# The last output block in two PSUM banks, and its rows stored in other pieces

## The chip, the cores and the metric

The kernel runs on one core of a Trainium2 chip. The metric is the device time of one execution in microseconds (us); lower is better. Three executions of the kernel before took 184.32, 182.17 and 182.27 us: median 182.27, lowest 182.17, highest 184.32. One further execution was taken with the hardware profiler; it is the one whose trace is read here.

A core has a matrix engine (TensorE, in the profile PE for matmuls and PEld for weight loads), three engines for elementwise work (VectorE is DVE, ScalarE is ACT, GpSimd is POOL), a queue engine (SyncE, SP) and 16 DMA engines that move data between the chip's memory and the core's SBUF. TensorE writes to PSUM, eight banks of 2 KB on each of 128 partitions; VectorE or ScalarE copies results from there to SBUF, and a DMA stores them. Each engine works through its own queue in order, and they wait for one another through semaphores. SP and ACT each issue DMAs on a queue of their own: SP's is q1 in the profile, ACT's is q10.

## The reference

Sigmoid attention over 8 batches of 12 heads with 448 positions of 64 elements, and behind it a token mixer over the joined heads (448 x 768 for each batch):

```python
scores = scale * np.matmul(q, k.transpose(0, 1, 3, 2)) - np.log(S)
attn = 1.0 / (1.0 + np.exp(-scores))
x = np.matmul(attn, v)                      # then (B, S, H * D) = (8, 448, 768)
wq = x @ w_q                                # 768 -> 64
wk = x @ w_k
W_tok = scale * np.einsum('bsd,btd->bst', wq, wk)
mixed = np.einsum('bst,btd->bsd', W_tok, x)
out = np.maximum(mixed, 0.0) @ w_out        # 768 x 768
```

All inputs and the output are float32. The kernel computes in bfloat16 and accumulates in float32.

## The kernel before

**Stages.** The work is cut into 24 groups `n`, each one batch `u` with four heads. For a group, q, k and v are loaded as float32 (`load1`), cast to bfloat16 (`cast1`, on POOL, DVE or ACT, line 202 for v), and q and k are turned so that the head's 64 elements lie on partitions. `scores(n, i)` makes one seventh of a group's scores (line 298) and their sigmoid on ACT (line 303); `values(n, i)` multiplies with v (line 320), where each weight load reads 64 columns of the cast v tile. Three groups make up a batch. Then follow the projections (`mlp_wqk`, lines 383 and 395), transposes, the mixer's products (`mlp_tmp`, `mlp_mix`) with the relu, and the output product with `w_out`.

**Output.** Two batches make a pair `w` (0 to 3). The pair's 896 rows are cut into seven blocks `m` of 128 rows. An output row of batch b has the number 7 p + i, with p from 0 to 63 and i from 0 to 6; a block holds two values of i, one on partitions 0 to 63 and one on partitions 64 to 127. So a store of one i takes 64 partitions, and its rows in memory lie 7 rows apart. Three functions write output: `out_pair` (pairs 1 and 2), `out_halves` (tokens I and i, blocks 0 to 2 of the last pair) and `out_chunk` (the others). `out_chunk` makes a block's 768 columns in two halves of 384 (`nb` 0 and 1, `NB` = 384), each in one PSUM bank, by six matmuls over the six slices of 128 of the inner dimension (line 590). A half is made in two calls of three matmuls each: the first leaves its state in `opened`, the second (`part` 1) finishes it, copies the bank to the SBUF tile `o` (line 614, on ACT where the token is o or Q, else on DVE), and after the second half the block is stored by `store`: two DMAs of 64 rows (line 599), the first on SP, the second on ACT in the tail of the kernel (`tail`: all scores are done).

**The last block.** For block 6 of pair 3, `split` holds: each half of 384 columns is stored by itself as soon as it is copied. For its second half, the bank is copied in two parts of 192 columns, one on DVE (line 611) and one on ACT (line 612). Both read the same bank, and the framework makes the second wait for the first. Then both 64-row pieces of 384 columns are stored, one on SP and one on ACT.

**Order.** The order of the work is written out by hand: one letter per step in the string `PLAN`. It ends in sixteen tokens O, o and Q, four for each of the last pair's blocks 3 to 6. `BANKS` is a second string that gives, in the order of the requests, the PSUM banks that each step takes (`bank1`, `bank2`); an assertion at the end wants all of it used. The last eight entries, 2 3 4 5 6 7 0 1, are the eight halves of blocks 3 to 6. `read` records who reads a bank, and with `keep=True` two engines that read one bank stay ordered. The `o` tiles come from a pool of three buffers, so block 6 takes the buffer of block 3 after that block's stores have landed.

**Loads and casts.** `ORDER` lists the loads; a dot or a capital letter marks a cast that goes to DVE or ACT at a place fixed in `PLAN`, the others go to POOL as soon as they may (`pump`). Of the 24 casts of v, 20 run on POOL and four on DVE. The tile of a cast v is laid out as partition, seventh `i`, head pair `b`, 64 elements; the float32 tile it comes from as partition, head pair, seventh, 64 elements.

Of the kernel before, what the change touches and what calls it, by code (L numbers as in the profile page):

```python
# [10 lines left out]
BF16 = mybir.dt.bfloat16  # L11
# [6 lines left out]
def kernel(  # L18
# [12 lines left out]
    nc = tc.nc  # L31
    B, H, S, HD = q.shape
    D = H * HD
    DH = moe_w_q.shape[1]
    assert DH == HD == 64 and S == 448 and D == 768
    P = 128
    NI, NP = 7, 64
    NU = B
    NJ = H // 4
    NC = D // P  # L40
    NB = D // 2
    HALF = (slice(0, 64), slice(64, 128))
# [5 lines left out]
    def pool(name, bufs, **kw):  # L48
        return ctx.enter_context(tc.tile_pool(name=name, bufs=bufs, **kw))
# [3 lines left out]
    p_c16 = pool("c16", 2)  # L53
    p_v16 = pool("v16", 4)
# [24 lines left out]
    )  # L79
    BANKS = BANKS.split()[::-1]  # L80

# [2 lines left out]
    def take(*ids):  # L84
        for b in ids:
            readers[b] = (readers[b][0] + readers[b][1], [])

    def bank2():
        lo, hi = (int(b) for b in BANKS.pop())
        take(lo, hi)  # L90
        assert hi == lo + 1
        return (lo, hi), banks[:, lo : hi + 1], banks16[:, lo : hi + 1]

    def bank1():
        b = int(BANKS.pop())
        take(b)
        return (b,), banks[:, b], banks16[:, b]

    def read(fb, inst, keep=False):

        for b in fb:
            for old in readers[b][0]:
                if not keep and old.ins.engine != inst.ins.engine:
                    tc.declare_no_dep(inst.ins, old.ins, reason="both only read the bank")
            readers[b][1].append(inst)
# [15 lines left out]
    quads = [(u, j) for u in range(NU) for j in range(NJ)]  # L121
    N = len(quads)
    COPY = dict(v=nc.vector.tensor_copy, s=nc.scalar.copy, g=nc.gpsimd.tensor_copy)

    def xt(u, j):
        return xts[u % 2 * NJ + j]
# [20 lines left out]
    ld = {}  # L147
# [39 lines left out]
    def cast1(n, nm, e):  # L187
        if KIND[n] in "cer" and nm != "v":
            if n not in pq:
                pq[n] = p_c16.tile([P, 2, 2, NI, 32, 2], BF16, tag="qk16", name="qk16")  # L190
            f = pq[n]
            COPY[e](  # L192
                out=f[:, :, "qk".index(nm)].rearrange("p e i d y -> p e y i d"),
                in_=ld.pop((nm, n)).rearrange("p (y i e d) -> p e y i d", y=2, i=NI, e=2),
            )
            ld[nm + "16", n] = f
            if ("q16", n) in ld and ("k16", n) in ld:
                arrange(n, nc.gpsimd)
            return
        p = p_v16 if nm == "v" else p_c16  # L200
        t16 = p.tile([P, NI, 2, HD], BF16, tag=nm + "16", name=nm + "16")
        COPY[e](  # L202
            out=t16.rearrange("p i b d -> p b i d"),
            in_=ld.pop((nm, n)).rearrange("p b (i d) -> p b i d", i=NI),
        )
        ld[nm + "16", n] = t16
# [106 lines left out]
    def values(n, i, tail, eng):  # L313
        u, j = quads[n]
        if i == 0:
            pv[n] = bank2()
        fb, ps, _ = pv[n]
        for h in range(2):
            for g in range(2):
                nc.tensor.matmul(  # L320
                    ps[HALF[g], h, 0:S], ld["v16", n][HALF[h], i, g, :],
                    ats[n, i][HALF[h], g, :], start=(i == 0), stop=(i == NI - 1),
                )
        if i == NI - 1:
            if tail:
                for h in range(2):
                    read(fb, COPY["vs"[h]](out=xt(u, j)[:, h, 0:S], in_=ps[:, h, 0:S]))
            else:
                read(fb, COPY[eng](out=xt(u, j)[:, :, 0:S], in_=ps[:, :, 0:S]))  # L329
# [158 lines left out]
    chunks = []  # L488
    ot = {}

    opened = []
# [80 lines left out]
    def out_chunk(act, tail):  # L572

        if opened:
            w, m, nb, fb, ps = opened.pop()
            part = 1
        else:
            w, m, nb = chunks.pop(0)
            if nb < 0:
                nb = 0  # L580
                chunks.insert(0, (w, m, 1))
            fb, ps, _ = bank1()
            part = 0
        if nb == 0 and not part:
            ot[0] = p_o.tile([P, D], F32, tag="o", name="o")
        o = ot[0]

        def block(ps, w0, w1, c0, c1):
            for c in range(c0, c1):
                nc.tensor.matmul(  # L590
                    ps, mxs[w][:, 2 * S * c + m * P : 2 * S * c + (m + 1) * P],
                    wout16[:, c, w0:w1], start=(c == 0), stop=(c == NC - 1),
                )

        def store(cols):
            for y in range(2):
                b, i = divmod(2 * m + y, NI)
                eng = nc.scalar if tail and y else nc.sync
                eng.dma_start(
                    out=out[2 * w + b].rearrange("(p i) d -> p i d", i=NI)[:, i, cols],  # L600
                    in_=o[HALF[y], cols],
                )

        ps = ps[:, 0:NB] if not part else ps
        block(ps, nb * NB, (nb + 1) * NB, part * NC // 2, (part + 1) * NC // 2)
        if not part:
            opened.append((w, m, nb, fb, ps))
            return
        if w == NU // 2 - 1 and not chunks:
            h = NB // 2  # L610
            read(fb, nc.vector.tensor_copy(out=o[:, NB : NB + h], in_=ps[:, 0:h]), keep=True)
            read(fb, nc.scalar.copy(out=o[:, NB + h :], in_=ps[:, h:]), keep=True)
        else:
            read(fb, COPY["s" if act else "v"](out=o[:, nb * NB : (nb + 1) * NB], in_=ps), keep=True)  # L614
        split = tail and w == NU // 2 - 1 and m == NI - 1
        if nb or split:
            store(slice(nb * NB, (nb + 1) * NB) if split else slice(0, D))

    w32 = {}

# [21 lines left out]
    def cols(r):  # L642
        return slice(r.start * HD, r.stop * HD)
# [8 lines left out]
        out=ident, in_=ident, compare_op=ALU.not_equal, fill=1.0, base=0,  # L652
# [8 lines left out]
    for t in wqks:  # L661
        nc.vector.memset(t[:, S:], 0.0)


    ORDER = (
# [4 lines left out]
    )  # L670
    BY = {"s": [], "v": []}
    for x in ORDER.split():
        if x[0] == ".":
# [1 line left out]
        elif x[0].isupper():  # L675
            BY["s"].append((x[0].lower(), int(x[1:])))
    OTHERS = set(BY["s"] + BY["v"])
    ORDER = [(x[0], int(x[1:])) for x in ORDER.replace(".", "").lower().split()]
    done = dict.fromkeys("SPqkKxWNUMOCgz", 0)
    used, loaded, cast = set(), set(), set()  # L680

# [2 lines left out]
    def pump_loads():  # L684
        while len(loaded) < len(ORDER):
            nm, n = ORDER[len(loaded)]
            if nm == "w" and n:
                loaded.add((nm, n))
                continue
            if len(ring) >= 8 and ring[-8] not in cast:  # L690
                break
            ring.append((nm, n))
            if nm == "w":
                load_weights()
            else:
                load1(n, nm, nc.sync)
            loaded.add((nm, n))
# [13 lines left out]
    def cast_now(nm, n, e):  # L711
        if nm != "w":
            cast1(n, nm, e)
        elif n:
            if n % 3 == 1:
                load_wout(n - 1)
        else:
            for h in range(2):
                for g in range(2):
                    COPY[e](  # L720
                        out=wqk16[HALF[g], h::2],
                        in_=w32["qk"].rearrange("p (c n) -> p c n", c=NC)[HALF[h], g::2],
                    )
        cast.add((nm, n))
        pump_loads()
# [3 lines left out]
    def pump():  # L729
        while pumped[0] < len(ORDER):  # L730
            nm, n = ORDER[pumped[0]]
            if (nm, n) not in OTHERS:
                if not ready(nm, n):
                    break
                cast_now(nm, n, "g")
            pumped[0] += 1

    def cast_next(e):
# [7 lines left out]
    for t16, t32, r, e in ((q016, q0, IA, "v"), (q016, q0, IB, "s"), (k016, k0, KA, "g"), (k016, k0, KB, "g")):  # L746
        COPY[e](
            out=t16[:, r].rearrange("p i b d -> p b i d"),
            in_=t32[:, :, cols(r)].rearrange("p b (i d) -> p b i d", d=HD),
# [23 lines left out]
    for t in PLAN:  # L773
# [9 lines left out]
        tail = done["S"] == N * NI  # L783
        if t == "S":
            scores(*divmod(c, NI))
        elif kind == "P":
            n, i = divmod(c, NI)
            values(n, i, tail or t == "R", "s" if t == "p" else "v")
            if i == NI - 1:
                used.add(("v", n))  # L790
                pump()
# [13 lines left out]
        elif t == "z":  # L805
            n = quads_r.pop(0)
# [16 lines left out]
        elif kind == "M":  # L823
            u, x = divmod(c, NC // 2)
# [44 lines left out]
```

## Time and profile before

| | |
|---|---|
| median of 3 runs | 182.27 us |
| the profiled execution's own time | 182.05 us |
| its span, first to last instruction | 180.3 us |
| granted TensorE clock, mean | 0.996 |
| TensorE, ScalarE, VectorE, GpSimd busy | 169.6, 160.0, 142.1, 123.4 us |
| last matmul of the run, end (modelled) | 176.13 us |
| read from memory, written to memory | 35.78 MB, 11.01 MB |

The span is some 1.8 us shorter than the time of the same execution; the rest lies ahead of the first and behind the last instruction. Busy shares are means over the whole run. The chain of waits goes back from the last instruction, at each step to what released it. For a DMA the profile has the time at which its queue issued it, the time until its data had landed, and for each queue the packets: one for each row moved and some small ones that report completion.

### The profile page before, as it was taken

Reading aid. Unit: us, or ns where it says so; the run is one execution under the profiler, and the core shown is the slowest. Engines: PE = TensorE matmul, PEld = TensorE weight load, DVE = VectorE, ACT = ScalarE, POOL = GpSimd, SP = SyncE. Lnnn points to the kernel's source line nnn. Section 1 sums busy time; section 2 is a strip of 40 time slices with the busy share of each in tenths; the row PEclk is TensorE's granted clock in tenths of the full one; section 3 lists DMA queues with packets and bytes.
Section 4 is the critical chain, followed back from the end, with each engine's and each line's share of the span. In section 5 each row is a group of like instructions: output and inputs, shape, how many; then the busy total and the mean of one; then the engine's idle time right before and its main releaser. Section 6 shows DMA issues by size and latency. Waiting matters only on the chain.

```text
span 180.3 us, 7970 instructions
## 1 busy us (share of the span) xinstructions
PE 169.6 (94%) x3471; PEld 112.5 (62%) x3472; DVE 142.1 (79%) x229; ACT 160.0 (89%) x212; POOL 123.4 (68%) x168
## 2 busy tenths in 40 slices
PE   7787899889999999999999999999999999999990
PEld 7333555554455445655686768778987789778560
DVE  3239599998989899889899879887999866588810
ACT  4699999999999999999999989999999899985240
POOL 1397799998998999999999999989306990000000
PEclk9999999999999999999999999999999999999998
DMA  5999999999999799989998999983946744442686
GB/s 174 356 394 387 331 382 376 288 302 364 411 340 346 181 306 292 372 285 288 313 282 285 281 374 346 316 266 96 264 118 155 226 95 107 91 91 46 157 241 175
DMA packets 24915, 47.31 MB, mean 262 GB/s; under 512 B 3888, under 2 KB 18480, under 8 KB 24880
## 3 DMA queue, kind: packets, MB, share of 16 engines
q1 hardware_dynamic: 23680, 44.84, 77.0%
q0 software_dynamic: 800, 1.18, 3.6%
q10 hardware_dynamic: 400, 0.79, 1.4%
q8 instruction: 27, 0.44, 1.0%
q14 instruction: 8, 0.07, 0.1%
HBM read 35.78 MB, written 11.01 MB: 260 GB/s over the span
## 4 chain that ended last, share of the span: by engine, by line
PE 67%; DVE 14%; DMA 9%; POOL 4%; SPq 2%; ACT 2%; issue 2%
PE banks L298 13%; PE banks L320 13%; PE banks L590 13%; PE banks L509 11%; DVE qk L232 4%; DMA k<-in_k_dram 4%; DMA v<-in_v_dram 3%; PE banks L549 3%; PE banks L395 3%; DVE xt L329 3%; POOL qk L192 3%; PE banks L358 2%; DVE qk L256 2%; DVE xn L347 1%; DMA out_dram<-o 1%
## 5 line engine op out<-in xcount | busy, mean ns | idle before, releaser
L303 ACT ACTIVATE at<-banks 128x896 bf16<-128x896 f32 x168 | 140.9, 946 | 3.6 <-PE banks L298 2.7
L298 PE MATMUL banks<-qk 64*64 64x448 bf16 x672 | 62.5, 357 | 2.5 <-DVE xt L329 1.4
L320 PE MATMUL banks<-at,v 64*64 64x448 bf16 x672 | 46.5, 350 | 0.1
L298 PEld LDWEIGHTS <-qk 64*64 64x64 bf16 x672 | 25.8, 105 | 21.1 <-issue 12.5
L509 PE MATMUL banks<-wout,mx 64*64 64x384 bf16 x672 | 36.3, 323 | 0.0
L320 PEld LDWEIGHTS <-v 64*64 64x64 bf16 x672 | 23.7, 106 | 6.9 <-issue 0.8
L509 PEld LDWEIGHTS <-mx 64*64 64x64 bf16 x672 | 23.3, 107 | 4.3
L590 PE MATMUL banks<-wout,mx 128*128 128x384 bf16 x132 | 24.8, 327 | 0.0
L192 POOL CAST qk<-q 128x896 bf16<-128x896 f32 x19 | 22.6, 1191 | 0.7 <-DMA q<-in_q_dram 0.2
L450 DVE TENSOR_SCALAR mx<-banks 128x512 bf16<-128x512 f32 (+3 forms) x24 | 21.0, 882 | 2.4 <-PE banks L477 1.6
L161 POOL COPY swap<-qk 32x448 uint32<-32x448 uint32 x28 | 15.8, 564 | 10.2 <-DVE qk L192 8.5
L192 POOL CAST qk<-k 128x896 bf16<-128x896 f32 x18 | 21.5, 1194 | 1.8 <-POOL qk L167 0.9
L329 DVE CAST xt<-banks 128x896 bf16<-128x896 f32 x19 | 20.5, 1081 | 1.4 <-PE banks L320 1.0
L202 POOL CAST v<-v 128x896 bf16<-128x896 f32 x20 | 18.4, 931 | 0.6
L590 PEld LDWEIGHTS <-mx 128*128 128x128 bf16 x132 | 11.9, 98 | 10.7 <-issue 3.9
L164 POOL COPY qk<-qk 32x448 uint32<-32x448 uint32 x28 | 16.6, 592 | 1.6
L263 DVE STREAM_TRANSPOSE qk<-qk 128x448 f32<-128x448 f32 x28 | 17.3, 630 | 0.1
L167 POOL COPY qk<-swap 32x448 uint32<-32x448 uint32 x28 | 15.8, 564 | 1.6
L232 DVE STREAM_TRANSPOSE qk<-qk 32x448 f32<-32x448 f32 x24 | 15.3, 636 | 0.6
L371 DVE COPY xn<-banks 128x1024 bf16<-128x1024 bf16 (+1 forms) x17 | 11.1, 654 | 4.6 <-PE banks L358 4.6
L614 DVE COPY o<-banks 128x384 f32<-128x384 f32 x15 | 8.2, 550 | 1.6 <-PE banks L590 0.8
L358 PEld LDWEIGHTS <-xt 64*64 64x64 bf16 x544 | 7.6, 109 | 1.9 <-issue 1.0
(87 smaller groups left out, 196.2 us busy)
## 6 DMA issues: line engine op xcount, KB each, us to landing
q<-in_q_dram SPq DMA_DIRECT2D x24, 448.0 KB, 7.0
v<-in_v_dram SPq DMA_DIRECT2D x24, 448.0 KB, 6.3
k<-in_k_dram SPq DMA_DIRECT2D x23, 448.0 KB, 7.3
out_dram<-o SPq DMA_DIRECT2D x51, 192.0 KB, 3.5
wout<-in_moe_w_out_dram POOLq DMA_DIRECT2D x2, 576.0 KB, 12.1
wout<-wout SPq DMA_DIRECT2D x12, 96.0 KB, 5.2
out_dram<-o ACTq DMA_DIRECT2D x3, 192.0 KB, 3.4
k<-in_k_dram SPq DMA_DIRECT2D x1, 256.0 KB, 5.2
```

The lines of the kernel that those rows point to most:

```text
L164: eng.tensor_copy(out=w[hi, 0], in_=w[lo, 1])
L192: COPY[e](out=f[:, :, "qk".index(nm)].rearrange("p e i d y -> p e y i d"), in_=ld.pop((nm, n)).rearrange("p (y i e d) -> p e y i d", y=2, ...
L202: COPY[e](out=t16.rearrange("p i b d -> p b i d"), in_=ld.pop((nm, n)).rearrange("p b (i d) -> p b i d", i=NI),)
L232: nc.vector.transpose(out=qk[n][other : other + 32, h].rearrange("p t i n -> p (t i n)").bitcast(F32), in_=w[own : own + 32, 1 - h],)
L263: nc.vector.transpose(out=qk[n][:, t].rearrange("p t i n -> p (t i n)").bitcast(F32), in_=w)
L298: nc.tensor.matmul(sc[HALF[h], g, 0:S], qk[n][HALF[g], h, 1, i, :], qk[n][HALF[g], h, 0].rearrange("p i n -> p (i n)"), start=True, stop=True,
L303: inst = nc.scalar.activation(at, sc[:, :, 0:S], ACTF.Sigmoid, bias=attn_bias, scale=attn_scale)
L320: nc.tensor.matmul(ps[HALF[g], h, 0:S], ld["v16", n][HALF[h], i, g, :], ats[n, i][HALF[h], g, :], start=(i == 0), stop=(i == NI - 1),)
L329: read(fb, COPY[eng](out=xt(u, j)[:, :, 0:S], in_=ps[:, :, 0:S]))
L450: inst = nc.vector.tensor_scalar(dst, ps, moe_scale, 0.0, ALU.mult, ALU.max)
L509: nc.tensor.matmul(ps[HALF[x], y, 0:NB], mx[HALF[y], u, b, 64 * (i - 3 * y) : 64 * (i - 3 * y) + 64], wout16[HALF[y], slot(y, b), x * NB : ...
L590: nc.tensor.matmul(ps, mxs[w][:, 2 * S * c + m * P : 2 * S * c + (m + 1) * P], wout16[:, c, w0:w1], start=(c == 0), stop=(c == NC - 1),)
```

## The change

The tile of a cast v is now laid out as partition, head pair, seventh, 64 elements, as its source is. `cast1` writes it in one run, and line 320 reads it with the two indices exchanged. `cast1` also gets a way to load v with a DMA that casts, for entries of `ORDER` marked with a star. No entry has a star, so it isn't used.

The last block's second half takes two banks: the string `BANKS` gets one more entry, 2. Its first call makes columns 384 to 575 with all six slices, and its second call columns 576 to 767 with all six. DVE copies the first bank, ACT the second, without waiting for each other.

The stores of the last block's rows: columns 0 to 383 and columns 384 to 575 are each stored by one DMA on SP for all 128 partitions (`store_both`), whose destination counts the two values of i, then 64 rows, then the columns. Columns 576 to 767 are stored by two DMAs of 64 rows, on SP and on ACT. In all, ACT issues one store fewer and SP one more; the order of all other instructions on all engines is as before.

```diff
-        "45 01 67 45 01 2 3 4 5 6 7 0 1 "
+        "45 01 67 45 01 2 3 4 5 6 7 0 1 2 "
...
-        p = p_v16 if nm == "v" else p_c16
-        t16 = p.tile([P, NI, 2, HD], BF16, tag=nm + "16", name=nm + "16")
+        if nm == "v":
+            t16 = p_v16.tile([P, 2, NI, HD], BF16, tag="v16", name="v16")
...
+                COPY[e](
+                    out=t16.rearrange("p b i d -> p (b i d)"), in_=ld.pop((nm, n)).rearrange("p b x -> p (b x)"),
+                )
+            ld["v16", n] = t16
+            return
...
-                    ps[HALF[g], h, 0:S], ld["v16", n][HALF[h], i, g, :],
+                    ps[HALF[g], h, 0:S], ld["v16", n][HALF[h], g, i, :],
...
+        last = w == NU // 2 - 1 and m == NI - 1
+
+        def store_both(cols):
+
+            b, i = divmod(2 * m, NI)
+            nc.sync.dma_start(
+                out=out[2 * w + b].rearrange("(p i) d -> i p d", i=NI)[i : i + 2, :, cols], in_=o[:, cols],
+            )
...
+        if nb and last:
+
+            if part:
+                fb, ps, _ = bank1()
+            h = NB // 2
+            c0 = NB + part * h
+            block(ps[:, 0:h], c0, c0 + h, 0, NC)
+            read(fb, COPY["vs"[part]](out=o[:, c0 : c0 + h], in_=ps[:, 0:h]), keep=True)
+            if part:
+                store(slice(c0, D))
+            else:
+                store_both(slice(c0, c0 + h))
+                opened.append((w, m, nb, fb, ps))
+            return
...
-        if w == NU // 2 - 1 and not chunks:
-            h = NB // 2
-            read(fb, nc.vector.tensor_copy(out=o[:, NB : NB + h], in_=ps[:, 0:h]), keep=True)
-            read(fb, nc.scalar.copy(out=o[:, NB + h :], in_=ps[:, h:]), keep=True)
-        else:
-            read(fb, COPY["s" if act else "v"](out=o[:, nb * NB : (nb + 1) * NB], in_=ps), keep=True)
-        split = tail and w == NU // 2 - 1 and m == NI - 1
-        if nb or split:
-            store(slice(nb * NB, (nb + 1) * NB) if split else slice(0, D))
+        read(fb, COPY["s" if act else "v"](out=o[:, nb * NB : (nb + 1) * NB], in_=ps), keep=True)
+        if last:
+            store_both(slice(0, NB))
+        elif nb:
+            store(slice(0, D))
```

More of the change, by code (lines that the diff above doesn't have):

```diff
@@ L199, in cast1 @@
             return
-        p = p_v16 if nm == "v" else p_c16
-        t16 = p.tile([P, NI, 2, HD], BF16, tag=nm + "16", name=nm + "16")
+        if nm == "v":
+            t16 = p_v16.tile([P, 2, NI, HD], BF16, tag="v16", name="v16")
+            if e == "d":
+                u, j = quads[n]
+                nc.gpsimd.dma_start(
+                    out=t16.rearrange("p b i d -> p b (i d)"),
+                    in_=v[u, 4 * j : 4 * j + 4].rearrange("(g h) (p i) d -> (h p) g (i d)", g=2, i=NI),
+                )
[5 more added lines that the diff above has]
+            return
+        t16 = p_c16.tile([P, NI, 2, HD], BF16, tag=nm + "16", name=nm + "16")
         COPY[e](
@@ L593, in block @@
                 )
+        last = w == NU // 2 - 1 and m == NI - 1
[3 more added lines that the diff above has]
+                out=out[2 * w + b].rearrange("(p i) d -> i p d", i=NI)[i : i + 2, :, cols], in_=o[:, cols],
+            )
         def store(cols):
@@ L602, in store @@
                 )
+        if nb and last:
[7 more added lines that the diff above has]
+                store(slice(c0, D))
+            else:
+                store_both(slice(c0, c0 + h))
+                opened.append((w, m, nb, fb, ps))
+            return
         ps = ps[:, 0:NB] if not part else ps
@@ L677 @@
     OTHERS = set(BY["s"] + BY["v"])
-    ORDER = [(x[0], int(x[1:])) for x in ORDER.replace(".", "").lower().split()]
+    CASTING = {("v", int(x[2:])) for x in ORDER.split() if x[0] == "*"}
+    ORDER = [(x[0], int(x[1:])) for x in ORDER.replace(".", "").replace("*", "").lower().split()]
     done = dict.fromkeys("SPqkKxWNUMOCgz", 0)
@@ L686, in pump_loads @@
             nm, n = ORDER[len(loaded)]
-            if nm == "w" and n:
+            if nm == "w" and n or (nm, n) in CASTING:
                 loaded.add((nm, n))
@@ L734, in pump @@
                     break
-                cast_now(nm, n, "g")
+                cast_now(nm, n, "d" if (nm, n) in CASTING else "g")
             pumped[0] += 1
```

## The prediction

> **What bounds the kernel now.** I read the page first, for the engine that fills the span.
>
> ```profile
> span 180.3 us, 7970 instructions
> ...
> PE 169.6 (94%) x3471; PEld 112.5 (62%) x3472; DVE 142.1 (79%) x229; ACT 160.0 (89%) x212; POOL 123.4 (68%) x168
> ...
> q10 hardware_dynamic: 400, 0.79, 1.4%
> ```
>
> TensorE is busy for 94% of the span, so in the middle of the run only something that delays or feeds TensorE counts. The change touches the end, so next comes the chain of waits, its last five pieces (start, duration, what):
>
> ```profile
> 168.21 7.92 PE banks L590 x48
> 176.13 0.02 issue
> 176.15 0.37 DVE o L611
> 176.52 0.02 issue
> 176.54 0.32 ACT o L612
> ```
>
> The last 48 matmuls run back to back, 7.92 / 48 = 0.165 us each. Then VectorE and ScalarE copy the two halves of one PSUM bank one after the other. After that only stores are left. When they are issued is in ScalarE's timeline and in line 599's own answer (durations in ns, first and last start):
>
> ```profile
> 175.38 0.48 ACT L614 COPY o<-banks 128x384 f32<-128x384 f32 x1 [0.70 <-DMA out_dram<-o]
> 175.89 0.50 ACTq L599 DMA_DIRECT2D out_dram<-o  x1
> ```
>
> ```profile
> L599 SPq DMA_DIRECT2D out_dram<-o x1: 467/467/467, 176.9 to 176.9; - x1
> L599 ACTq DMA_DIRECT2D out_dram<-o x1: 497/497/497, 176.9 to 176.9; - x1
> ```
>
> Both queues issue a 64-row piece of the left half at 175.89 and of the right half at 176.89. The DMA answers for 177.0 to 177.5 and 177.5 to 178.0 show how long those take to land, and what the queues moved:
>
> ```profile
> DMA packets 75, 0.17 MB, mean 335 GB/s; under 512 B 14, under 2 KB 27, under 8 KB 75
> ...
> q10 hardware_dynamic: 58, 0.15, 82.5%
> q1 hardware_dynamic: 17, 0.02, 11.0%
> issues: line engine op xcount, KB each, median us to landing
> out_dram<-o SPq DMA_DIRECT2D x1, 96.0 KB, 2.2
> out_dram<-o ACTq DMA_DIRECT2D x1, 96.0 KB, 2.5
> ```
>
> ```profile
> DMA packets 126, 0.16 MB, mean 320 GB/s; under 512 B 22, under 2 KB 126, under 8 KB 126
> ...
> q10 hardware_dynamic: 61, 0.08, 46.3%
> q1 hardware_dynamic: 65, 0.08, 44.2%
> ```
>
> The last piece lands at 176.89 + 2.5 = 179.39, and the span ends 0.9 us later. So the set end is: copies, an issue, 2.5 us of DMA, 0.9 us of closing. The stages by time agree; their last two columns are the share of 16 DMA engines and GB/s:
>
> ```profile
> 178.00:179.00 1.00, 0.00 (x0) 0.00 (x0) 0.00 (x0) 0.00 (x0) 0.00 (x0) 0.94 0.70 214
> 179.00:180.30 1.30, 0.00 (x0) 0.00 (x0) 0.00 (x0) 0.00 (x0) 0.00 (x0) 0.50 0.00 0
> ```
>
> Data moves until about 179.0, and 0.4 us later the last piece has landed.
>
> **The change, part by part.** The sum is made against the profiled execution, 182.05 us around its span of 180.3; the median of the runs, 182.27, is 0.22 above it.
>
> *The v tile.* The 24 casts of v now write one run of 896 elements where they wrote fourteen of 64. The groups, shapes kept apart (busy us, mean ns of one | idle):
>
> ```profile
> L202 POOL CAST v<-v 128x896 bf16<-128x896 f32 x20 | 18.4, 931 | 0.6
> ...
> L202 DVE CAST v<-v 128x896 bf16<-128x896 f32 x4 | 2.8, 696 | 0.0
> ...
> L404 POOL COPY wq<-wqk 64x448 bf16<-64x448 bf16 x4 | 2.2, 555 | 0.2
> ...
> L747 POOL CAST k<-k 128x512 bf16<-128x512 f32 x1 | 0.6, 613 | 1.7 <-DMA k<-in_k_dram 1.7
> ```
>
> On POOL a copy in one run (555 ns for 448) and a cast in runs of 64 (613 for 512) lie on a line with the 931 for 896: 613 + 384 x (613 - 555) / 64 = 961. The shape of the run does not show in the price, so I take nothing; the 30 ns between line and row, twenty times, is 0.6 us either way, on an engine with 57 us to spare. VectorE's four casts could gain at most a part of 4 x 0.70 = 2.8 us, beside TensorE's work; nothing taken. TensorE's weight loads still read 64 elements in a row.
>
> *The last 384 columns.* Six matmuls of 384 columns become twelve of 192, with six more weight loads. Nothing of 192 columns was run; the nearest below is the transposes of 128 columns with the same 128 x 128 load:
>
> ```profile
> 38.35 0.57 PE banks L342 x8
> ```
>
> That is 0.071 us each. By columns twelve cost 12 x 0.165 / 2 = 0.99 us, exactly the old six; by the line through 0.071 and 0.165 they cost 12 x 0.0945 = 1.13. So 0 to +0.15; I take +0.07. Bank 2, the second bank, was emptied by the row block three before, so its wait costs nothing.
>
> *The copies.* VectorE's 0.37 us now lies under the second six matmuls, and ScalarE's 0.32 follows TensorE directly: 176.13 + 0.07 + 0.02 + 0.32 = 176.54 instead of 176.86. That is 0.32 us earlier, and the ScalarE queue issues its last piece, now 64 x 192, at 176.57.
>
> *The stores.* ScalarE's issue at 175.89 goes (0.50 us of its queue, which waited for nothing). On SP three follow one another: 2 x 64 rows of 384 columns after the copy that ends at 175.86, 2 x 64 rows of 192 columns after VectorE's copy (about 176.1), and 64 rows of 192. SP's price for an issue with two dimensions beside the columns:
>
> ```profile
> L563 SPq DMA_DIRECT2D out_dram<-o x6: 595/598/1222, 164.5 to 170.2; - x6
> ```
>
> So the issues start at 175.89, 176.54 and 177.19: the last is 0.30 us later than SP's last was (176.89), and whoever waits for SP is the end of the program alone.
>
> What decides is how the two new stores are carried. Their destination counts 2 rows outermost, then 64, then the columns; every store of before counts 64 outermost. ScalarE's queue shows how such a one is divided: 400 packets for five stores are 80 each, 64 rows and 16 completions, one for each of 16 engines that took four rows. An issue costs SP 0.47 us for 64 rows and 0.60 for 64 x 2, far too little to deal out rows singly, so I take it that the outermost dimension is cut into equal shares. Of two there are two shares: **two engines carry 64 rows each, and 14 stand idle.** No row of this trace has an outermost count below 64, so this is inferred, and its bounds are 16 engines (below) and two.
>
> The Trainium skill states this as a rule (DMA: Bandwidth & Descriptors, section "Why a DMA increments its semaphore by 16 and not by 1"): the number of engines is the largest up to 16 that divides the slowest dimension of both access patterns. For 2 and 128 that is two engines; no run shown so far has tried it.
>
> The price of a row: from 177.5 to 178.0 the two queues took (46.3 + 44.2)% of 16 x 0.5 us = 7.24 us for 126 - 22 = 104 rows of 1,536 bytes, 70 ns each. In the half before, 93.5% of 8 us is 7.48; less 13 such rows, 48 rows of 3,072 bytes took 6.57 us, 137 ns each. The price goes by bytes, 22 GB/s per engine, and the line through both gives 36 ns for 768 bytes. On each of the two engines:
> - the first rows of 1,536 bytes ran between 177.0 and 177.5, after an issue at 175.89 and behind the row block before: start about 177.2
> - 64 x 0.070 = 4.5 us, to 181.7
> - the second store behind it, 64 x 0.036 = 2.3 us, to 184.0
> - its share of SP's last piece, 4 x 0.036 = 0.15, to 184.2
> - 0.4 to landing, 0.9 of closing: the span ends at 185.5.
>
> That is 5.2 us later; the 0.32 us from the copies is lost under it, since the first store's issue at 175.89 has not moved. 182.05 + 5.2 = 187.25, and with the median's 0.22 about **187.5 us**.
>
> Bounds of the row's price: the fastest slice of the page and the store queue alone.
>
> ```profile
> GB/s 174 356 394 387 331 382 376 288 302 364 411 340 346 181 306 292 372 285 288 313 282 285 281 374 346 316 266 96 264 118 155 226 95 107 91 91 46 157 241 175
> ```
>
> ```profile
> q1 hardware_dynamic: 1408, 1.94, 45.4%
> ```
>
> 411 / 16 = 25.7 GB/s puts 147,456 bytes through in 5.7 us instead of 6.8: 186.4. The second line is from 141 to 160 us, where SP alone stores: 45.4% of 16 x 19 us = 138 us for 1.94 MB, 14 GB/s. Then it is 10.5 us, 3.7 more: 191.2. I stay with 22: each of those stores reads 64 partitions with all 16 engines, while two queues over 128 partitions reached 335 GB/s.
>
> **The rivals.**
>
> *Sixteen engines carry the two-row stores as all others.* For it: every store measured used 16. Against it: none had this form. Then the ScalarE queue lands at 176.57 + 2.5 = 179.07 and SP at 177.19 + 2.2 = 179.39, which is the old landing; half the bytes per piece may take 0.2 off. 0 to -0.3: 182.2 us, not slower. It decides if the first store lands within about 3 us.
>
> *Sixteen engines, but the SP queue becomes the bound.* SP carries 344 KB of the last 393. At the 14 GB/s per engine of SP alone, 225 GB/s, these need 1.53 us from 177.2, to 178.7, beneath the 179.39; issues of 0.75 instead of 0.60 would add 0.3. So 182.5 us. In the Trainium skill (DMA: Bandwidth & Descriptors, "Rules for kernel authors") two transfers of disjoint partition halves are said to gain nothing over one of 128 partitions, which by itself would make this merge free; the 335 against 225 GB/s differ from that.
>
> *Two engines at SP's lone rate*: 191.2 us, as worked out. For it: only one queue feeds them. Against: at 3,072 bytes as at 1,536 time went by bytes, so no fixed wait per row shows.
>
> **How the numbers follow.** Two engines at 22 to 26 GB/s, the forecast: 0.68. Two engines near 14 GB/s: 0.13. Sixteen engines: 0.13. SP bound: 0.06. The likeliest gives 187.5. The range takes in the forecast with its bounds (186.4, and 0.5 less if the start and the landing are each somewhat shorter) and most of the slow case: 185.9 to 191.3. Within 2% of 182.27 (up to 185.9, about what a measurement of this kernel can tell from no change) are the two cases of sixteen engines, 0.19, less a hundredth; faster by that much is out of reach of a tail whose copies are worth 0.3 us: 0.01. Slower: 0.80.
>
> **What would show it.** Right: the two two-row stores land after some 6 and 8 us instead of 2.7, the DMA share falls to about 2/16 after 178.5, SP's closing wait for the stores grows from about 1 us to 6 or more, and ScalarE's last copy starts right after TensorE at about 176.2. Wrong: all landings near 2.5 us, or a slowdown that stands ahead of 175.9, where v's new layout would have cost what I put at nothing.

## The result, and the profile after

The changed kernel takes 188.62 us (median of 6 runs, 187.92 to 190.58), the kernel before 182.22 in the same series: a ratio of 1.0349, 95% interval 1.0279 to 1.042. It is slower by 6.4 us. Ratios here and below come from the runs outside a kernel's slower state, so they need not be the quotient of the two medians beside them. The execution that was profiled took 187.92 us, the fastest of the six, 5.87 more than the profiled one of before.

The head of the page of the changed kernel, and its rate of DMA in 40 slices of 4.65 us:

```profile
span 186.1 us, 7984 instructions
...
PE 169.9 (91%) x3478; PEld 113.5 (61%) x3478; DVE 142.7 (77%) x229; ACT 159.8 (86%) x212; POOL 123.9 (67%) x168
...
GB/s 177 397 384 371 350 384 341 302 298 404 386 311 279 271 289 345 312 314 306 302 262 301 327 331 321 284 75 288 105 179 214 95 85 92 88 85 174 238 69 30
```

No engine's busy time has grown by more than 1.0 us (169.6 to 169.9 us on TensorE), and the last two slices move 69 and 30 GB/s where the kernel before ended with 241 and 175. To see that the time is lost in the tail alone, take the start of the last four row blocks' matmuls, first before, then after (start, duration):

```profile
168.14 7.97 PE L590 MATMUL banks<-wout,mx 128*128 128x384 bf16 x48
```

```profile
167.83 7.99 PE L603 MATMUL banks<-wout,mx 128*128 128x384 bf16 x54
```

The changed kernel gets there 0.3 us earlier. From there to the end of the span it is 180.3 - 168.14 = 12.16 us before and 186.1 - 167.83 = 18.27 after: the tail is 6.1 us longer. This length, called the tail below, is what the experiments are read by, since the start of the tail itself moves from run to run: in the traces here it lies between 167.83 and 170.09 us.

The end of the timeline after (start, duration, engine; SPq and ACTq are issues):

```profile
175.08 0.48 ACT L645 COPY o<-banks 128x384 f32<-128x384 f32 x1 [0.70 <-DMA out_dram<-o]
175.37 0.36 DVE L633 COPY o<-banks 128x192 f32<-128x192 f32 x1 [3.65 <-PE banks L603]
175.58 1.24 SPq L613 DMA_DIRECT2D out_dram<-o  x2
175.86 0.32 ACT L633 COPY o<-banks 128x192 f32<-128x192 f32 x1 [0.30 <-PE banks L603]
176.21 0.47 ACTq L621 DMA_DIRECT2D out_dram<-o  x1
176.92 0.70 SPq L621 DMA_DIRECT2D out_dram<-o  x1
```

The copies do what the change says: ScalarE's last one waits for TensorE and starts 0.78 us after its copy of the left half; before it was 1.16 us (176.54 - 175.38). All is issued by 177.6. From there to the end of the span only DMAs run. The stages by time (last two columns: share of 16 engines, GB/s), then the landings of the last small pieces (KB, us from issue to landing) and SP's closing wait:

```profile
177.00:178.00 1.00, 0.00 (x0) 0.00 (x0) 0.00 (x0) 0.00 (x0) 0.00 (x0) 1.00 0.51 48
178.00:179.00 1.00, 0.00 (x0) 0.00 (x0) 0.00 (x0) 0.00 (x0) 0.00 (x0) 0.82 0.60 59
179.00:180.00 1.00, 0.00 (x0) 0.00 (x0) 0.00 (x0) 0.00 (x0) 0.00 (x0) 0.50 0.61 76
180.00:181.00 1.00, 0.00 (x0) 0.00 (x0) 0.00 (x0) 0.00 (x0) 0.00 (x0) 0.50 0.31 56
181.00:182.00 1.00, 0.00 (x0) 0.00 (x0) 0.00 (x0) 0.00 (x0) 0.00 (x0) 0.50 0.13 48
182.00:183.00 1.00, 0.00 (x0) 0.00 (x0) 0.00 (x0) 0.00 (x0) 0.00 (x0) 0.50 0.14 47
183.00:184.00 1.00, 0.00 (x0) 0.00 (x0) 0.00 (x0) 0.00 (x0) 0.00 (x0) 0.50 0.14 48
184.00:185.00 1.00, 0.00 (x0) 0.00 (x0) 0.00 (x0) 0.00 (x0) 0.00 (x0) 0.50 0.06 21
```

```profile
out_dram<-o ACTq DMA_DIRECT2D x1, 48.0 KB, 3.9
out_dram<-o SPq DMA_DIRECT2D x1, 48.0 KB, 8.1
```

```profile
SPq L897 <- DMA out_dram<-o: 7.3, 1, 7.3
```

From 181 to 184 the share is 0.13 to 0.14, and 2/16 is 0.125: two engines at work, with 47 to 48 GB/s together. Between 178 and 180 it is still 0.6, and yet only 59 to 76 GB/s move: the small last pieces, which all engines carry, run slowly there too. SP's last piece, 48 KB, lands at 176.92 + 8.1 = 185.0. It stands behind the two-row stores on two of the engines. SP waits 7.3 us for it at the end, where it was 1.7 in two waits.

### The profile page after: what moved, and what is told of

It reads as the page before. It is cut to its first block, busy times and chain, and to the rows that moved or that the text cites. A ratio compares the mean times of both kernels' runs of the same rounds, so it can differ in the third digit from the quotient of the medians.

```text
span 186.1 us, 7984 instructions
## 1 busy us (share of the span) xinstructions
PE 169.9 (91%) x3478; PEld 113.5 (61%) x3478; DVE 142.7 (77%) x229; ACT 159.8 (86%) x212; POOL 123.9 (67%) x168
## 4 chain that ended last, share of the span: by engine, by line
PE 57%; POOL 15%; DVE 11%; ACT 8%; issue 2%; DMA 2%; SPq 0%; POOLq 0%; DVEq 0%
PE banks L311 11%; PE banks L333 11%; PE banks L522 10%; PE banks L603 10%; ACT at L316 7%; POOL qk L192 5%; DVE qk L245 3%; PE banks L562 3%; POOL swap L161 3%; POOL qk L167 3%; POOL qk L164 2%; DVE xt L342 2%; PE banks L408 2%; PE banks L371 2%; DMA k<-in_k_dram 2%
## 5 line engine op out<-in xcount | busy, mean ns | idle before, releaser
L311 PEld LDWEIGHTS <-qk 64*64 64x64 bf16 x672 | 26.4, 105 | 21.3 <-issue 13.1
L603 PE MATMUL banks<-wout,mx 128*128 128x384 bf16 (+1 forms) x138 | 24.8, 320 | 0.0
```

What stands on the lines that cost most here:

```text
L311: nc.tensor.matmul(sc[HALF[h], g, 0:S], qk[n][HALF[g], h, 1, i, :], qk[n][HALF[g], h, 0].rearrange("p i n -> p (i n)"), start=True, stop=True,
L603: nc.tensor.matmul(ps, mxs[w][:, 2 * S * c + m * P : 2 * S * c + (m + 1) * P], wout16[:, c, w0:w1], start=(c == 0), stop=(c == NC - 1),)
```

## The experiments

The theory: each two-row store is carried by two of 16 engines, since its destination counts 2 outermost. The rivals: the SP queue is the bound, because it issues and carries almost all; the new layout of v costs; the order in which rows reach memory costs.

### The two-row stores taken apart

```diff
...
         def store_both(cols):
-            b, i = divmod(2 * m, NI)
-            nc.sync.dma_start(
-                out=out[2 * w + b].rearrange("(p i) d -> i p d", i=NI)[i : i + 2, :, cols], in_=o[:, cols],
-            )
+            for y in range(2):
+                b, i = divmod(2 * m + y, NI)
+                nc.sync.dma_start(
+                    out=out[2 * w + b].rearrange("(p i) d -> p i d", i=NI)[:, i, cols], in_=o[HALF[y], cols],
+                )
```

> The changed kernel, with each two-row store taken apart into two stores of 64 rows, both on SP; v's layout, the two banks and ScalarE's part stay. If two engines carried the two-row stores: the loss of 6 us goes, and SP's five issues in a row (some 0.5 us each from 175.6) put its last one at about 177.8, some 0.9 us later than in the kernel before; with 2.2 us to land and 0.9 of closing the time is 182.3 to 183.2. If the SP queue with most of the bytes is what costs: still 186 or more, since the same bytes go through the same queue. If v's layout costs: unchanged, 188.

Measured: 183.91 us against 183.3 of before on that chip, ratio 1.0059 (1.002 to 1.0099). The tail is 181.9 - 168.27 = 13.63 us. Of the 6.1 us, 4.6 are gone, with the same bytes still on the SP queue. By the times some 1.1 us over before are left (0.4 to 1.8 by the interval; 0.1 to 1.0 was expected). SP's row of issues fits that:

```profile
176.02 2.66 SPq L614 DMA_DIRECT2D out_dram<-o  x4
178.77 0.55 SPq L622 DMA_DIRECT2D out_dram<-o  x1
```

Its fifth issue starts 2.75 us after its first; before, the second was the last, 1.0 us after the first (176.89 - 175.89). So the rival of the SP queue is worth 1.5 us of tail at most, in this one trace, and it isn't the cause of the 6.

### v's layout alone, and two banks alone

```diff
...
-        t16 = p.tile([P, NI, 2, HD], BF16, tag=nm + "16", name=nm + "16")
+        if nm == "v":
+            t16 = p_v16.tile([P, 2, NI, HD], BF16, tag="v16", name="v16")
...
-                    ps[HALF[g], h, 0:S], ld["v16", n][HALF[h], i, g, :],
+                    ps[HALF[g], h, 0:S], ld["v16", n][HALF[h], g, i, :],
```

> The kernel before with v's tile in the new layout and nothing else. By the prediction: no difference, 182.2 within 0.3, POOL's cast of 896 elements stays at 931 ns within 10. Rival: VectorE's four casts of v, which had a mean of 696 ns before and 858 in the changed kernel, are slower by the layout; then they show 850 again here, and the time may be up to 0.6 us longer.

Measured: ratio 1.0002 (0.9966 to 1.0039), tail 180.5 - 168.37 = 12.13 us against 12.16. No difference shows, within 0.7 us either way.

```profile
L202 POOL CAST v<-v 128x896 bf16<-128x896 f32 x20 | 18.3, 931 | 0.7 <-DMA v<-in_v_dram 0.2
...
L202 DVE CAST v<-v 128x896 bf16<-128x896 f32 x4 | 2.8, 700 | 0.0
```

VectorE's four casts have 700 ns here with the new layout, 858 in the changed kernel, and 849 in the run with one two-row store below, which has the old layout: the spread isn't the layout's.

```diff
-        "45 01 67 45 01 2 3 4 5 6 7 0 1 "
+        "45 01 67 45 01 2 3 4 5 6 7 0 1 2 "
...
+        if nb and last:
+            if part:
+                fb, ps, _ = bank1()
+            h = NB // 2
+            c0 = NB + part * h
+            block(ps[:, 0:h], c0, c0 + h, 0, NC)
+            read(fb, COPY["vs"[part]](out=o[:, c0 : c0 + h], in_=ps[:, 0:h]), keep=True)
+            if part:
+                store(slice(NB, D))
...
```

> The kernel before with the last half of the last block in two PSUM banks and nothing else: the copies run side by side, and the stores are as before (64 rows, 384 columns, one each on SP and ACT). By the working of the prediction the last issue comes 0.3 us earlier, so 181.9 against 182.2, at most 0.4 less, and the wait of ScalarE's last copy is for TensorE and no longer for VectorE. If twelve matmuls of 192 columns cost more than by columns, up to 0.15 of it goes. If the end is set by the DMA engines and not by the last issue: no difference.

> The kernel with two banks and the stores of before once more, since its gain of 0.3 us lay within the uncertainty: a ratio of 0.998 is expected again, with an interval that together with the first tells it from 1 or does not.

Measured: ratios 0.9977 (0.9937 to 1.0016) and 0.9995 (0.9962 to 1.0028); the tails are 182.1 - 170.09 = 12.01 and 181.1 - 168.88 = 12.22 us against 12.16. The tails show no gain of 0.3 us; the times can't tell 0.3 us, or 0.16%, from nothing. ScalarE's timeline in the first of the two shows what became of it:

```profile
177.33 0.48 ACT L627 COPY o<-banks 128x384 f32<-128x384 f32 x1 [0.70 <-DMA out_dram<-o]
177.84 0.50 ACTq L599 DMA_DIRECT2D out_dram<-o  x1
178.38 0.32 ACT L611 COPY o<-banks 128x192 f32<-128x192 f32 x1 [0.57 <-PE banks L590]
```

With the stores of before, ScalarE's own queue issues a piece of the left half between its two copies, until 178.34, and the last copy starts at 178.38, 1.05 us after the first (in the second run it is 1.05 too). Without that issue, in the changed kernel, it was 0.78, before it was 1.16. The profile puts the wait down to TensorE, but the issue ended last. So the wait between the copies hid an issue, and taking the wait away moves the last copy by only 0.1 us unless the issue goes elsewhere too.

A version in which ScalarE copies the first bank and each queue stores 192 columns behind each copy runs into the same issues (its edit, set against the run with two banks):

```diff
...
-            read(fb, COPY["vs"[part]](out=o[:, c0 : c0 + h], in_=ps[:, 0:h]), keep=True)
-            if part:
-                store(slice(NB, D))
+            read(fb, COPY["sv"[part]](out=o[:, c0 : c0 + h], in_=ps[:, 0:h]), keep=True)
+            store(slice(c0, c0 + h))
...
```

> The kernel before with two banks, ScalarE copying the first and VectorE the second, and 64 rows of 192 columns stored from each queue behind each copy. The last stores are issued at about 176.6, 0.3 us earlier than before, and are half as large. If the end follows the last issue: 181.6 to 181.9. If small rows cost the DMA engines more than their bytes (36 ns for 768 bytes was taken), the gain shrinks to none.

Measured: ratio 0.9993 (0.995 to 1.0036), tail 181.6 - 168.92 = 12.68 us, half a microsecond longer, with one issue more on each queue. The 0.3 to 0.6 us that it was expected to win aren't there. No version here beats the kernel before by more than the uncertainty.

### One two-row store, and one on each queue

```diff
...
+            if split and not nb:
+                b, i = divmod(2 * m, NI)
+                nc.sync.dma_start(
+                    out=out[2 * w + b].rearrange("(p i) d -> i p d", i=NI)[i : i + 2, :, 0:NB], in_=o[:, 0:NB],
+                )
+                return
```

> The kernel before with only the left half of the last block in a two-row store on SP; the right half as before. With two engines: 98 KB on each at the 24 GB/s that the changed kernel shows are 4.1 us from about 177.2, then four rows of the last piece, 0.3: data until 181.6, landing and closing 1.3 to 1.5, span 183 and time 184.6 to 185.2. With sixteen engines: 182.2.

Measured: 186.31 against 183.01, ratio 1.0184 (1.013 to 1.0238): 3.3 us for one such store, somewhat above the 2.4 to 3.0 over 182.2 that was expected. Tail 184.4 - 168.41 = 15.99. A two-row store does it with v, the banks and the copies of before.

```diff
-        def store_both(cols):
+        def store_both(cols, eng=nc.sync):
...
-            nc.sync.dma_start(
+            eng.dma_start(
...
-            store_both(slice(0, NB))
+            store_both(slice(0, NB), nc.scalar)
```

> The changed kernel with its first two-row store (384 columns) issued from ACT and the second from SP. If two of the engines carry every two-row store, whichever queue it comes from, the same two have the same 147 KB each: 187.5 to 189, no gain. If one queue's rate is the bound, or each queue has engines of its own, the two stores run side by side: the 2.1 us of the second go, about 186.3. If SP's issue is what costs: about 183.

Measured: 189.04 against 183.01, ratio 1.0311 (1.0237 to 1.0386), as slow as the changed kernel. Tail 187.8 - 169.25 = 18.55. With one two-row store on each queue, two of the late microseconds, and the packets of each queue from 183.0 to 183.5, are:

```profile
183.00:184.00 1.00, 0.00 (x0) 0.00 (x0) 0.00 (x0) 0.00 (x0) 0.00 (x0) 0.50 0.14 50
184.00:185.00 1.00, 0.00 (x0) 0.00 (x0) 0.00 (x0) 0.00 (x0) 0.00 (x0) 0.50 0.13 47
```

```profile
q10 hardware_dynamic: 11, 0.02, 8.9%
q1 hardware_dynamic: 11, 0.01, 5.0%
```

Both queues move rows then, and together they fill 13.9% of 16 engines, about two of them (12.5%): both queues' stores share the same two engines. A queue's own rate isn't the bound.

### The outermost count as the only change

```diff
-                eng.dma_start(
-                    out=out[2 * w + b].rearrange("(p i) d -> p i d", i=NI)[:, i, cols],
-                    in_=o[HALF[y], cols],
-                )
+                dst = out[2 * w + b].rearrange("(p i) d -> p i d", i=NI)[:, i, cols]
+                if tail and w == NU // 2 - 1 and m == NI - 1:
+                    dst = dst.rearrange("(x a) d -> a x d", a=4)
+                eng.dma_start(out=dst, in_=o[HALF[y], cols])
```

Three more runs have 8, 16 and 2 in the place of the 4.

> The kernel before; in the last block's four stores the 64 rows go to memory in another order (so the rows of that block stand at other places), such that the destination counts 4 outermost and then 16. Bytes, queues, issue times and row lengths are those of before. If the outermost count is the number of engines: four engines carry 393 KB, 98 KB each, 4.1 us from about 177.2 at 24 GB/s: span 182.5 to 183, time 184.3 to 185. If the order of rows in memory is what costs, or nothing does: 182.2 to 182.6.

> As the run with 4 outermost, with 8 outermost and then 8. If the outermost count is the number of engines: 49 KB on each of eight, 2.05 us from 177.2, data until about 179.3 instead of 179.0: time 182.3 to 182.9, and in the last microseconds the DMA share does not go above a half. If the count does not matter: as before, with a share of 0.9 or more.

> As the runs with 4 and 8 outermost, with 16 outermost and then 4, so the rows of the last block stand in another order in memory. If the outermost count sets the number of engines: sixteen, and time and DMA share are those of the kernel before (span 180 to 181 from equal ends of TensorE, share 0.9 in the microsecond after the last block's first rows). If the order of the rows in memory costs by itself: longer by 0.5 or more, as with 8.

> The same with 2 outermost and then 32: four stores of 64 rows, two from each queue. All 393 KB of the last block then go through two engines, 197 KB each, 8.2 us at 24 GB/s, and some 1 us for the slow start: data until 186.5, span 187.8 to 188.5, time 189.5 to 190.3. In the last microseconds the DMA share is 0.13 and the rate 48 GB/s.

Each was timed once, so the tail and the late rates tell more than the times. The rates with 2 outermost, with 4, with 8 and with 16, a line or two from each run's stages:

```profile
183.00:184.00 1.00, 0.00 (x0) 0.00 (x0) 0.00 (x0) 0.00 (x0) 0.00 (x0) 0.50 0.13 49
```

```profile
182.00:183.00 1.00, 0.00 (x0) 0.00 (x0) 0.00 (x0) 0.00 (x0) 0.00 (x0) 0.50 0.23 66
183.00:184.00 1.00, 0.00 (x0) 0.00 (x0) 0.00 (x0) 0.00 (x0) 0.00 (x0) 0.50 0.24 88
```

```profile
178.00:179.00 1.00, 0.00 (x0) 0.00 (x0) 0.00 (x0) 0.00 (x0) 0.00 (x0) 0.99 0.40 135
179.00:180.00 1.00, 0.00 (x0) 0.00 (x0) 0.00 (x0) 0.00 (x0) 0.00 (x0) 0.50 0.48 146
```

```profile
178.00:179.00 1.00, 0.00 (x0) 0.00 (x0) 0.00 (x0) 0.00 (x0) 0.00 (x0) 1.00 0.76 258
```

| outermost | time, us | tail, us | late share | count / 16 | GB/s per engine at work |
|---|---|---|---|---|---|
| 2 | 192.18 | 190.4 - 169.68 = 20.72 | 0.13 | 0.125 | 49 / 2 = 24 |
| 4 | 187.53 | 185.8 - 169.38 = 16.42 | 0.24 | 0.25 | 88 / 4 = 22 |
| 8 | 183.61 | 181.8 - 168.11 = 13.69 | 0.48 | 0.5 | 146 / 8 = 18 |
| 16 | 183.0 | 181.2 - 168.97 = 12.23 | 0.76 | 1 | 258 / (0.76 x 16) = 21 |

The same bytes and rows on the same queues: the edits differ in the outermost count alone, and the share of engines at work follows it up to 8; with 16 the last rows no longer keep all engines busy. The packets of ScalarE's queue (q10) over the whole run count the engines directly. With 2, 4, 8 and 16 outermost the pages have:

```profile
q10 hardware_dynamic: 372, 0.79, 1.1%
```

```profile
q10 hardware_dynamic: 376, 0.79, 1.1%
```

```profile
q10 hardware_dynamic: 384, 0.79, 1.2%
```

```profile
q10 hardware_dynamic: 400, 0.79, 1.2%
```

Three of this queue's five stores are unchanged and have 80 packets each, 64 rows and 16 completions. The other two have the rest: 372 - 240 = 132, which is 2 x (64 + 2), then 2 x (64 + 4), 2 x (64 + 8) and 2 x (64 + 16). A store leaves as many completions as its outermost count, and 16 where that is 64; read as the prediction read them, one for each engine that took part.

With 16 the tail is that of before (12.23 against 12.16), though its rows too reach memory in another order, so another order by itself cost nothing there. The Trainium skill's rule (DMA: Bandwidth & Descriptors, section "Why a DMA increments its semaphore by 16 and not by 1"), the largest number up to 16 that divides the slowest dimension of both sides, agrees with all four rows.

With 2, 4 and 8 the times came out 1.9, 2.5 and 0.7 us above the top of what was expected; the kernel before took 183.0 to 183.15 in these series, some 0.8 to 0.9 more than the 182.2 us of the first series, which is one part of it. Another part is ScalarE's issue, which takes 1.35 us with 4 outermost and 0.50 before, ahead of its last copy; that copy starts 1.91 us after the one before it (178.53 - 176.62), where it was 1.16. The rest is not worked out.

```profile
177.13 1.35 ACTq L602 DMA_DIRECT2D out_dram<-o  x1
178.53 0.32 ACT L612 COPY o<-banks 128x192 f32<-128x192 f32 x1 [1.42 <-DVE o L611]
```

### A two-row store with nothing beside it

```diff
-        if nb or split:
-            store(slice(nb * NB, (nb + 1) * NB) if split else slice(0, D))
+        if split:
+            if nb:
+                b, i = divmod(2 * m, NI)
+                nc.sync.dma_start(
+                    out=out[2 * w + b].rearrange("(p i) d -> i p d", i=NI)[i : i + 2, :, :], in_=o,
+                )
+            return
+        if nb:
+            store(slice(0, D))
```

> The kernel before with all 768 columns of the last block in one two-row store on SP, issued when both halves are copied, and nothing behind it on either queue. 64 rows of 3,072 bytes on each of two engines, 128 ns each at 24 GB/s, are 8.2 us from 1.3 after the issue at about 176.9: data until 186.4, span about 187.8, time 189.6. In the runs so far a two-row store moved only half that rate in its first 2 us, while rows of other stores ran on the other engines. If those others hold it up, the rate is 48 GB/s here from the first microsecond on; if such a store always starts slowly, it is again near 25 at first and the time 190.5.

Measured, once: 189.88 us against 183.15 of before, tail 188.1 - 168.07 = 20.03. Its first microseconds, and the packets of SP's queue over the whole run, before and here:

```profile
178.00:179.00 1.00, 0.00 (x0) 0.00 (x0) 0.00 (x0) 0.00 (x0) 0.00 (x0) 0.71 0.15 25
179.00:180.00 1.00, 0.00 (x0) 0.00 (x0) 0.00 (x0) 0.00 (x0) 0.00 (x0) 0.50 0.10 31
180.00:181.00 1.00, 0.00 (x0) 0.00 (x0) 0.00 (x0) 0.00 (x0) 0.00 (x0) 0.50 0.14 43
181.00:182.00 1.00, 0.00 (x0) 0.00 (x0) 0.00 (x0) 0.00 (x0) 0.00 (x0) 0.50 0.12 49
```

```profile
q1 hardware_dynamic: 23680, 44.84, 77.0%
```

```profile
q1 hardware_dynamic: 23650, 45.03, 73.7%
```

On SP two stores of 80 packets went, and one came; 160 - 30 = 130 packets are its 128 rows and 2 completions. No other store is in flight from 178 on, and it still starts at half its later rate. Against 50 GB/s from the first, the three slow microseconds lack 25 + 19 + 7 = 51 KB, 1.0 us. That other stores hold it up is ruled out for this run; why such a store starts slowly stays open.

## Why the prediction was right

187.5 us was forecast and 188.62 measured; on the profiled executions, 5.2 us more against 5.87.

- **Two engines for the two-row stores.** Right, and shown from four sides: taken apart, 4.6 us of tail are gone; one of them alone costs 3.3 us; on two queues they are no faster; and the share and the number of completions follow the outermost count.
- **The price of a row.** 70 ns for 1,536 bytes and 36 for 768 were taken. The late rate of 48 GB/s makes it 1,536 / 24 = 64 ns and 32 ns. The slow case of 14 GB/s, which the queue's rate would have set, fell. The reason given against it was misread, though: in the half microsecond of 335 GB/s ScalarE's queue alone, with stores of 64 partitions, moved 0.15 of the 0.17 MB at 82.5% of the engines, which is 23 GB/s per engine. So reading 64 partitions does not by itself explain SP's 14, and what does stays open.
- **The term that was too small.** The stream was taken to run at full rate from its start. In the lone store it runs at 25, 31 and 43 GB/s in its first three microseconds, where 50 are reached later, and that costs 1.0 us. By the prediction's own clock the tail would have been 185.5 - 168.14 = 17.36, and it was 18.27, 0.9 more. The cheaper rows took 64 x (6 + 4) ns = 0.6 us off, so the sum lacked 1.5: about 1.0 for the slow start, if it is here what it is in the lone store, 0.2 for the closing (186.1 - 185.0 = 1.1 where 0.9 was taken), and 0.3 that is not accounted for. That the forecast came as near as it did is in part luck: two errors of opposite sign met.
- **The copies.** Forecast 0.32 us earlier by ScalarE, measured 1.16 - 0.78 = 0.38, hidden under the stores as forecast. The prediction credits it to the second bank; the run with two banks alone has 1.16 - 1.05 = 0.11, so most of it came from ScalarE's issue of 0.50 us, which was taken to hold up nothing and went to SP. Twelve matmuls of 192 columns cost nothing over six of 384: 54 matmuls in 7.99 us, 48 in 7.97. The allowance of 0.07 wasn't needed.
- **v's layout.** Taken at nothing, and nothing was measured (1.0002, within 0.7 us either way).
- **The SP queue.** Its rival was priced at 0.3 us over the old end; it is up to 1.5 us of tail once SP issues five 64-row stores in a row, and the prediction had three issues there. In the changed kernel it is covered.
- **The signs.** SP's closing wait of 7.3 us and ScalarE's copy right behind TensorE (175.86; the matmuls end at 167.83 + 7.99 = 175.82) came as said. The share of 2/16 came at 181 and not after 178.5: the prediction did not see how slowly ScalarE's last 48 KB would move beside the two-row stores; they took 3.9 us to land, where its last 96 KB took 2.5 before.

## What to carry to other kernels

Before merging two stores into one, look at the outermost count of its destination: here a store that counted 2, 4 or 8 first, with 64 to 8 rows beneath, left 14, 12 or 8 engines idle. (No run here varies the count of the source.) At the end of this kernel nothing hid that. And when a wait is removed, look at what the waiting engine issues in that time: here the wait of 0.3 us hid a DMA issue of 0.5 us, and nothing measurable was won while that issue stayed in its place. No run shows a faster kernel with the issue moved.

## What the runs showed of the hardware that was not expected

The lone two-row store starts slowly: 25, 31 and 43 GB/s in its first full microseconds, 49 to 55 after, with no other store in flight. Whether that comes of the few engines isn't shown. An issue can take longer as well: with 2, 4 or 8 outermost the first of ScalarE's two stores of the last block took 1.32 to 1.41 us to issue, 0.59 with 16, 0.50 before. The second one, of the same shape, took 0.55 to 0.65, so the count alone isn't the reason. And while the changed kernel's two-row stores ran, ScalarE's last 48 KB, spread over all 16 engines, took 3.9 us to land, where 48 KB took 2.0 in the run with all stores of 64 rows.
